# Sliding-window attention and a squared-ReLU FFN on one core: attention woven between the FFN's matmul groups, longer load runs for q and k, and the mask applied after the exponential

## Chip, cores, metric

The kernel runs on one core of a Trainium2 chip. The metric is the device time of one execution in microseconds (us). "Span" is the time from the first to the last instruction in one profiled execution; it is about 2 us shorter than the execution's time. PE is the tensor engine, DVE the vector engine, ACT the scalar engine, POOL the GpSimd engine, SP the engine that issues DMAs. The granted clock is the share of PE's full clock in the clock entries of a trace; where a trace has no entry, the views print 1.00.

## The reference

```python
# q, k, v: (8 batches, 8 heads, 576 tokens, 64), fp32, normal * 0.1
scores = q @ k.T / sqrt(64)
mask   = (0 <= i - j) & (i - j < 64)            # causal window of 64 keys
attn   = softmax(where(mask, scores, -1e9))
x      = (attn @ v) as (4608 tokens, 512)       # heads side by side
h      = maximum(x @ w_in, 0)                   # w_in  (512, 2048)
out    = (h * h) @ w_out                        # w_out (2048, 512), fp32 out
```

The inputs make the scores about 0.01 in size. So the softmax is nearly uniform, and the comparison with the reference hardly sees which query meets which key inside the window.

## The kernel before

A batch has four head pairs; two heads of 64 fill the 128 rows of the PE array. The FFN works on blocks of 512 tokens: "up" is 16 groups of four matmuls (hps), "down" is four groups of sixteen (ops). Each batch's attention is a stage of its own, followed by the FFN blocks whose tokens are then complete.

```python
# stageA(b, hp): load, cast, transpose, copy out of PSUM
for hh in range(2):
    nc.sync.dma_start(out=dst[:, 0:NC, hh, :],            # 64 floats = 256 B runs
        in_=src[b, h0 + hh, 0:NC * P, :].rearrange("(c p) d -> p c d", p=P))
    ...
nc.vector.tensor_copy(out=q16[:], in_=q_st[:])            # and k16: casts on DVE
... # 5 transposes each into qT_ps, kT_ps
nc.scalar.activation(out=qT[:], in_=qT_ps[:], func=AF.Copy, scale=1.0 / float(D) ** 0.5)
nc.scalar.activation(out=kT[:], in_=kT_ps[:], func=AF.Copy, scale=1.0)

# stageB: 18 score matmuls, then
nc.vector.tensor_tensor(out=pm[:, 0:512], in0=scA[hh][:], in1=mask_flat[:, 0:512], op=ALU.add)
nc.vector.tensor_tensor(out=pm[:, 512:S], in0=scB[hh][:], in1=mask_flat[:, 512:S], op=ALU.add)
nc.scalar.activation(out=pm[:], in_=pm[:], func=AF.Exp)
...
# main loop
for b in range(B):
    ctxs = [stageA(b, hp) for hp in range(HP)]
    if b == 0: load_w_in()                  # 16 x 256 KB through 3 staging buffers
    pms = [stageB(ctxs[hp]) for hp in range(HP)]
    for hp in range(HP): stageC(hp, ctxs[hp], pms[hp], x_sb)     # values, quotient
    if b == 0: load_w_out()
    ...                                     # transpose x into xT
    emit_ffn_blocks(ready)                  # the whole up stage, then the whole down stage
```

The softmax here doesn't subtract the row's maximum and nothing guards it: scores larger than these inputs give would overflow.

## Time and profile before

| | before |
|---|---|
| time, median of 3 runs | 444.27 us (444.19 to 444.62) |
| span of the profiled run | 443.0 us |
| attention of batch 2 complete | about 153.5 us |
| from there, one batch with one FFN block | 45.7 us |
| mean granted clock | 0.884 |

The 45.7 us come from the timeline: the first up matmul after batch 2's attention starts at 153.5 us and that after batch 7's at 382.0 us, five batches later. This start is what "attention complete" means for the kernel before. (The copy of the batch's last tokens into xT starts slightly later there, at 153.7 and 382.9 us, because the next block does not need them.)

From the page of the kernel before: busy time by engine; the granted clock in 40 slices of the span, in tenths; and the chain of waits by engine (the work that ended last, followed backwards).

```profile
PE 369.1 (83%) x2784; PEld 190.6 (43%) x2784; DVE 232.4 (52%) x648; ACT 217.3 (49%) x357; POOL 76.7 (17%) x241
...
PEclk9999999955999599967996799769975999599999
...
PE 61%; DVE 20%; DMA 7%; SPq 6%; issue 3%; ACT 1%; POOL 0%; DVEq 0%; POOLq 0%; ACTq 0%
```

PE looks 83% busy, but the clock row has a dip to 5 or 6 tenths once per batch. A "busy" PE at a low clock is not full speed. A batch cut into stages shows it. The next fence is the windows view: start and end of the stretch; its length; busy us of PE, PE weight load, DVE, ACT, POOL with the number of instructions; granted clock; share of the 16 DMA engines; GB/s.

```profile
core 0: us, PE busy (x) PEld busy (x) DVE busy (x) ACT busy (x) POOL busy (x), PEclk, DMA share, GB/s
138.00:153.50 15.50, 11.65 (x196) 8.52 (x196) 13.54 (x56) 10.55 (x19) 4.81 (x14) 0.67 0.56 132
153.50:169.00 15.50, 15.46 (x65) 6.67 (x65) 12.27 (x21) 9.76 (x16) 4.07 (x13) 0.89 0.54 123
169.00:184.00 15.00, 15.00 (x79) 7.07 (x78) 1.37 (x4) 4.67 (x8) 1.87 (x7) 1.00 0.56 145
```

The first stretch is attention: DVE is busy for 13.54 of 15.50 us, PE waits between small matmuls, and the clock is granted at 0.67. The second is the up stage, which starts at the low clock (0.89 on average); the third is mainly the down stage at full clock. The copies of the transposed q and k out of PSUM (busy us, mean ns of one, idle time before and its releaser):

```profile
L172 ACT ACTIVATE qT<-qT_ps 128x576 f16<-128x576 f16 x32 | 21.6, 675 | 19.3 <-PE qT_ps L164 19.3
L174 ACT ACTIVATE kT<-kT_ps 128x576 f16<-128x576 f16 x32 | 21.9, 685 | 8.1 <-PE kT_ps L164 8.1
```

### The profile page before, as it was taken

The page shows a single profiled execution, that of the slowest core. Times are in us where ns is not written, and L with a number is a line of the kernel's source. Part 1 is how long each engine was busy: PE and PEld are TensorE (multiplying, and loading weights), DVE is VectorE, ACT ScalarE, POOL GpSimd, SP SyncE. Part 2 cuts the span into 40 slices and gives each one's busy share as a digit, 9 for nine tenths or more (in the row PEclk, how much of TensorE's full clock was granted, in tenths as well). Part 3 has the DMA queues.
Part 4 walks back from the last instruction along what each step waited for, and adds up shares of the span by engine and source line. Part 5 has one row for each costly group of instructions (what it writes and reads, how often), then busy time and mean ns, then how long its engine had stood idle before and what let it go on. Part 6 is the DMA issues. An engine that isn't in the chain of part 4 may idle for free.

```text
span 443.0 us, 8064 instructions
## 1 busy us (share of the span) xinstructions
PE 369.1 (83%) x2784; PEld 190.6 (43%) x2784; DVE 232.4 (52%) x648; ACT 217.3 (49%) x357; POOL 76.7 (17%) x241
## 2 busy tenths in 40 slices
PE   1245698657999799969997999799988998899996
PEld 0133243343445444544455444534464445444442
DVE  0237780058823972396429751966088705788100
ACT  2233186652746465555537452826182717277311
POOL 5230201032312322232014200430011000000000
PEclk9999999955999599967996799769975999599999
DMA  4657888555556555645424532553130010000112
GB/s 112 138 131 203 228 217 232 165 133 115 122 133 164 122 122 132 170 108 117 117 83 111 121 82 83 122 117 70 71 80 0 2 68 28 1 1 1 47 72 73
DMA packets 126569, 46.68 MB, mean 105 GB/s; under 512 B 117824, under 2 KB 117824, under 8 KB 126528
## 3 DMA queue, kind: packets, MB, share of 16 engines
q1 hardware_dynamic: 126528, 46.17, 40.8%
q8 instruction: 22, 0.36, 0.3%
q14 instruction: 19, 0.16, 0.1%
HBM read 36.70 MB, written 9.44 MB: 104 GB/s over the span
## 4 chain that ended last, share of the span: by engine, by line
PE 61%; DVE 20%; DMA 7%; SPq 6%; issue 3%; ACT 1%; POOL 0%; DVEq 0%; POOLq 0%; ACTq 0%
PE hps L104 30%; PE ops L119 25%; DVE x_sb L251 4%; SPq L141 3%; SPq L146 3%; PE kT_ps L159 2%; DMA ws<-in_moe_w_in_dram 2%; DMA k_st<-in_k_dram 2%; PE qT_ps L159 2%; DVE x_sb L257 2%; DMA q_st<-in_q_dram 1%; DVE xT L284 1%; DVE rden L246 1%; ACT w_out_sb L94 1%; DMA ws_603<-in_moe_w_out_dram 1%
## 5 line engine op out<-in xcount | busy, mean ns | idle before, releaser
L104 PE MATMUL hps<-xT,w_in_sb 128*128 128x512 f16 x576 | 143.2, 416 | 5.2 <-DVE xT L284 5.1
L112 DVE TENSOR_SCALAR hrelu<-hps 128x512 f32<-128x512 f32 x144 | 99.1, 691 | 35.7 <-PE hps L104 33.1
L104 PEld LDWEIGHTS <-w_in_sb 128*128 128x128 f16 x576 | 60.6, 105 | 84.9 <-issue 27.9
L126 ACT ACTIVATE osb<-ops 128x512 f32<-128x512 f32 x36 | 21.3, 599 | 83.2 <-PE ops L119 83.2
L177 ACT ACTIVATE v_ev<-v_st 128x640 f16<-128x640 f32 x32 | 23.2, 730 | 27.8 <-DMA v_st<-in_v_dram 27.8
L182 POOL COPY v_od<-v_ev 64x512 f16<-64x512 f16 x32 | 19.5, 610 | 97.7 <-ACT v_ev L177 97.3
L278 PE MATMUL xt_ps<-ident,x_sb 128*128 128x128 f16 (+1 forms) x160 | 23.5, 293 | 11.0 <-DVE x_sb L251 6.0
L172 ACT ACTIVATE qT<-qT_ps 128x576 f16<-128x576 f16 x32 | 21.6, 675 | 19.3 <-PE qT_ps L164 19.3
L139 POOL MEMSET q_st<- 64x128 f32 x32 | 10.7, 334 | 98.2 <-DVE q_4818 L153 23.0
L174 ACT ACTIVATE kT<-kT_ps 128x576 f16<-128x576 f16 x32 | 21.9, 685 | 8.1 <-PE kT_ps L164 8.1
L202 PEld LDWEIGHTS <-kT 64*128 64x128 f16 x576 | 17.8, 104 | 12.0 <-issue 12.0
L278 PEld LDWEIGHTS <-x_sb 128*128 128x128 f16 (+1 forms) x160 | 14.0, 126 | 20.1 <-DVE x_sb L251 9.9
L184 POOL COPY v_od<-v_ev 64x512 f16<-64x512 f16 x32 | 19.7, 616 | 1.7
L119 PE MATMUL ops<-w_out_sb,h_654 128*128 128x512 f16 x64 | 15.0, 378 | 2.3 <-ACT w_out_sb L94 2.1
L114 ACT ACTIVATE h_3934<-hrelu 128x512 f16<-128x512 f32 x16 | 10.0, 630 | 11.1 <-DVE hrelu L112 10.9
L114 ACT ACTIVATE h_4590<-hrelu 128x512 f16<-128x512 f32 x16 | 10.1, 630 | 10.9 <-DVE hrelu L112 10.9
L114 ACT ACTIVATE h_5246<-hrelu 128x512 f16<-128x512 f32 x16 | 10.1, 630 | 10.6 <-DVE hrelu L112 10.6
L114 ACT ACTIVATE h_3278<-hrelu 128x512 f16<-128x512 f32 x16 | 10.0, 629 | 10.0 <-DVE hrelu L112 10.0
L119 PE MATMUL ops<-w_out_sb,h_5246 128*128 128x512 f16 x64 | 14.5, 379 | 0.0
L119 PE MATMUL ops<-w_out_sb,h_5247 128*128 128x512 f16 x64 | 14.5, 379 | 0.0
L139 POOL MEMSET k_st<- 64x128 f32 x32 | 9.4, 295 | 26.6 <-DMA v_st<-in_v_dram 3.3
L119 PE MATMUL ops<-w_out_sb,h_1310 128*128 128x512 f16 x64 | 14.0, 379 | 0.0
(1140 smaller groups left out, 615.1 us busy)
## 6 DMA issues: line engine op xcount, KB each, us to landing
out_dram<-osb SPq DMA_DIRECT2D x36, 256.0 KB, 2.0
q_st<-in_q_dram SPq DMA_DIRECT2D x64, 128.0 KB, 2.5
k_st<-in_k_dram SPq DMA_DIRECT2D x64, 128.0 KB, 2.4
v_st<-in_v_dram SPq DMA_DIRECT2D x64, 128.0 KB, 2.4
ws<-in_moe_w_in_dram SPq DMA_DIRECT2D x16, 256.0 KB, 4.1
q_st<-in_q_dram SPq DMA_DIRECT2D x64, 16.0 KB, 2.3
k_st<-in_k_dram SPq DMA_DIRECT2D x64, 16.0 KB, 2.2
v_st<-in_v_dram SPq DMA_DIRECT2D x64, 16.0 KB, 2.2
```

Of the source, the lines that this page charges most:

```text
L104: nc.tensor.matmul(hps[:], w_in_sb[:, c, f * P:(f + 1) * P], xT[:, c, g * 512:(g + 1) * 512], start=(c == 0), stop=(c == DMC - 1),)
L112: nc.vector.tensor_scalar(out=hrelu[:], in0=hps[:], scalar1=0.0, scalar2=None, op0=ALU.max)
L114: nc.scalar.activation(out=h2s[g][:, f, :], in_=hrelu[:], func=AF.Square)
L119: nc.tensor.matmul(ops_t[:], h2s[g][:, f, ts * P:(ts + 1) * P], w_out_sb[:, f, :], start=(f == 0), stop=(f == FFC - 1),)
L126: nc.scalar.activation(out=osb[:], in_=ops_t[:], func=AF.Copy, scale=OUT_SCALE)
L139: nc.gpsimd.memset(dst[TAIL:P, NC, :, :], 0.0)
L172: nc.scalar.activation(out=qT[:], in_=qT_ps[:], func=AF.Copy, scale=1.0 / float(D) ** 0.5)
L174: nc.scalar.activation(out=kT[:], in_=kT_ps[:], func=AF.Copy, scale=1.0)
L177: nc.scalar.activation(out=v_ev[:, :, :, 0:D], in_=v_st[:].rearrange("p c h d -> p h c d"), func=AF.Copy, scale=1.0,)
L182: nc.gpsimd.tensor_copy(out=v_od[0:64, :, :, 0:D], in_=v_ev[64:P, :, 0:NC, 0:D])
L184: nc.gpsimd.tensor_copy(out=v_od[64:P, :, :, 0:D], in_=v_ev[0:64, :, 1:NCH, 0:D])
L278: nc.tensor.transpose(out=xt_ps[:, c, 0:nrow], in_=x_sb[0:nrow, sc, c * P:(c + 1) * P], identity=ident[0:nrow, 0:nrow],)
```

## The change

The intent has three parts.

- **Weave.** The attention of batch g+1 is cut into steps, and they are emitted evenly between the up groups of block g and the down groups of block g-1. PE takes its matmuls in program order, so with this order it has FFN work between two dependent attention steps. PSUM is divided: three buffers for up, two for down, three for attention. The casts of q, k and v move to POOL, and q and k leave PSUM on ACT and DVE, one each.
- **Longer runs.** Partition p takes the six consecutive tokens 6p to 6p+5, so one run of q or k is 1.5 KB in place of 256 B. After the transposes the tokens stand as (r, p), and they must be (p, r). The copy out of PSUM does this: it reads contiguously and writes with a stride of six fp16 elements, 12 bytes.
- **Exponential first.** ACT takes exp straight from PSUM; then DVE takes the minimum with an fp16 mask (65504 to keep, 0 to drop), all in SBUF.

The rewrite changes more than the three parts named: the squared ReLU is now relu on ACT and a fused max and multiply on DVE (before: maximum on DVE, square on ACT), v is loaded for all eight heads at once, the last 64 queries of the four pairs are handled in one step, and the memsets of padding are gone.

The core of the diff; the old stages go, and the rest of the new code is left out ("..."):

```diff
+def weave(*streams):          # merge lists of steps evenly by relative position
+    keyed = []
+    for s, steps in enumerate(streams):
+        n = len(steps)
+        for i, step in enumerate(steps):
+            keyed.append(((i + 0.5) / n, s, i, step))
+    keyed.sort(key=lambda e: e[:3])
+    return [e[3] for e in keyed]
 ...
+    wst = ctx.enter_context(tc.tile_pool(name="wst", bufs=3))      # weight staging
+    ps_up  = ... bufs=3      ps_out = ... bufs=2      ps_att = ... bufs=3     (PSUM)
 ...
+                nc.sync.dma_start(                                 # 1.5 KB runs
+                    out=st[:].rearrange("p h r d -> p h (r d)"),
+                    in_=src[b, 2 * hp:2 * hp + 2].rearrange("h (p r) d -> p h (r d)", r=RT))
+                nc.gpsimd.tensor_copy(out=d16[:].rearrange("p r h d -> p h r d"), in_=st[:])
 ...
+                dT = attw.tile([P, PT, RT], FP16, name=f"{nm}T", tag=f"{nm}T", bufs=5)
+                if nm == "q":
+                    nc.scalar.activation(out=dT[:].rearrange("p t r -> p r t"), in_=ps[:],
+                                         func=AF.Copy, scale=1.0)
+                else:
+                    nc.vector.tensor_copy(out=dT[:].rearrange("p t r -> p r t"), in_=ps[:])
 ...
+                nc.scalar.activation(out=pm[:], in_=sc[hh][:], func=AF.Exp,
+                                     scale=1.0 / float(D) ** 0.5)
+                nc.vector.tensor_tensor(out=pm[:], in0=pm[:], in1=mask[:], op=ALU.min)
 ...
+        loads = [lambda hp=hp: load_qk(hp) for hp in range(HP)]
+        loads.insert(1, load_v)                                    # pair 0, all of v, pair 1 ...
+        for hp in range(HP):
+            steps.append(lambda hp=hp: transposes(hp))
+            steps.append(lambda hp=hp: scores(hp, pms[hp]))
+            if hp > 0:
+                steps.append(lambda hp=hp - 1: values(hp, pms[hp], holds[hp]))
+                steps.append(lambda hp=hp - 1: to_xT(hp, holds[hp]))
 ...
+    for g in range(NTB + 1):
+        streams = []
+        if g < NTB:    streams.append(ffn_up(g))
+        if g > 0:      streams.append(ffn_out(g - 1))
+        if g + 1 < B:  streams.append(nxt[1])                      # attention steps of g+1
+        if g == 0:     streams.append(w_out_steps)
+        if g + 2 < B:  nxt = attention(g + 2); streams.append(nxt[0])   # its loads
+        for s in weave(*streams):
+            s()
```

## The prediction

> **What bounds the kernel now.** The chain of waits is PE 61%, DVE 20%, DMA 7%. By stage windows, a steady batch takes about 46 us and alternates two stages. (a) Attention, 138.0 to 153.5 us: PE waits on DVE's mask adds (0.68 us each), quotients and copies; granted clock 0.67. (b) FFN, 153.5 to 184 us: PE-bound, 64 up matmuls in 15.5 us and 64 down matmuls in 13.8 us (216 ns each). The down stage runs at clock 1.00, the up stage at 0.84 to 0.89 because it starts cold. The Trainium skill ("TensorE: Matmul & The Clock Gate", Part 1) says that the array drops to half clock after an idle window and recovers after sustained work[...]. Around this: the first FFN matmul at 50 us, w_out waits to 82 us, and batch 1's attention only ending at 107 us (its chain waits for loads and POOL copies). SP issues 420 DMAs at 0.51 to 0.59 us each.
>
> **What the change does.**
> - Moves batch g+1's attention between the FFN matmul groups of blocks g and g-1. PE, in order, always has FFN work between dependent attention steps (about 1.7 us of it), so the 15.5 us stage shrinks to its pure PE time at full clock. From warm pieces of the trace: 18 score matmuls 0.29 us, 5 transposes 0.45 us, 16 value matmuls about 0.5 us (cold). That is 48 + 20 transposes about 6, 72 scores 1.3, 72 values 2.2: about 9.5 us per batch (estimate).
> - FFN at 216 ns throughout: 27.6 us per block, no cold up stage.
> - Exp straight from PSUM removes the serial DVE add before ACT; the fp16 min in SBUF should cost about 0.4 us against 0.68 (estimate, with the ratio of 16-bit SBUF tensor_tensor in "VectorE: DVE Perf Modes", perf-mode tier table; no trace yet shows it).
> - DVE per block about 24 us (now 27), ACT 20 to 21 (now 24.5), POOL up to about 18 (casts of q, k, v added, memsets gone): all well under PE.
> - DMA issues fall from about 420 to 124, most q/k packets from 256 B to 1.5 KB. The same bytes.
>
> **Sum.** Start: batch 0's loads (3.5 MB at 200 to 230 GB/s) and POOL casts give attention 0 done near 29 us; w_in, in rounds of three buffers, near 35. Block 0 and block 1 are still held by loads (18.9 MB, about 82 us at 230 GB/s) and w_out casts: block 1 ends near 100 us. Then five full blocks at 27.6 + 9.5 + about 5 for PE switches and in-order stalls = 42 (210), two FFN-only blocks at 28.2 (56), last down stage 14.7, last eviction and store 3: 384 us. The steady blocks give about 4 us each; the larger part comes from the first two batches (now attention 2 would end at 154 us, then near 100).
>
> **Prediction: 384 us, 8 in 10 between 368 and 404.** Faster by over 2%: 0.97; within 2%: 0.02; slower: 0.01.
>
> **What would show it.** Granted clock 0.95 or more from about 60 us on; PE idle under 10% in blocks 2 to 8; block period 40 to 44 us; the DVE share of the chain of waits below 8%; mean of both FFN matmul groups' spacing near 216 ns; exp near 0.6 us, min near 0.4 us; first FFN matmul near 25 to 30 us.
>
> **What would make it wrong.** Higher: stride-6 fp16 writes of qT/kT slow on ACT/DVE; POOL casts of 96x768 over 1.5 us, so that attention waits for POOL; three PSUM buffers for attention too few, so that every step stalls PE; batch 0's serial casts of v before q1/k1 delaying the start; weights' three staging buffers. Lower: attention's matmuls hidden better than estimated, loads faster than 230 GB/s.

## The result and the profile after

| | before | after |
|---|---|---|
| median of 4 runs | 444.23 us (444.00 to 444.62) | 382.96 us (382.22 to 383.91) |
| ratio, 95% interval | | 0.8628 (0.8609 to 0.8647): faster |
| span of the profiled run | 443.0 us | 380.5 us |
| mean granted clock | 0.884 | 0.994 |
| attention of batch 2 complete | 153.5 us | 120.7 us |
| one batch with one FFN block, later | 45.7 us | 37.4 us |

A ratio is the mean time of one kernel's fast runs over that of the other kernel's in the same rounds; it is not quite the ratio of the medians quoted beside it.

The same three lines of the page after, with the next line of the page, the chain by line of the program:

```profile
PE 327.2 (86%) x2848; PEld 160.5 (42%) x2848; DVE 255.4 (67%) x468; ACT 215.0 (56%) x309; POOL 118.6 (31%) x178
...
PEclk9999998999999999999999999999999999999999
...
PE 60%; DVE 23%; ACT 6%; DMA 4%; issue 3%; POOL 2%; SPq 0%; ACTq 0%; POOLq 0%
PE ops L307 25%; PE hps L288 23%; DVE kT L171 15%; DMA ws<-in_moe_w_in_dram 3%; PE av L204 2%; ACT hrelu L293 2%; DVE x_sb L209 2%; PE xt_ps L216 2%; PE qT_ps L164 2%; PE kT_ps L164 2%; DMA v_st<-in_v_dram 1%; ACT w_out_sb L123 1%; ACT qT L168 1%; DVE h_601 L294 1%; DVE w_in_sb L110 1%
```

The dips of the clock row are gone. PE's busy time fell from 369.1 to 327.2 us for practically the same matrix work. But one line is new in the chain: the DVE copy of kT, L171, with 15% of the span. The two copies, by group:

```profile
L168 ACT ACTIVATE qT<-qT_ps 128x576 f16<-128x576 f16 x32 | 67.4, 2105 | 29.3 <-PE qT_ps L164 29.2
L171 DVE COPY kT<-kT_ps 128x576 f16<-128x576 f16 x32 | 66.7, 2086 | 14.4 <-PE kT_ps L164 13.7
```

The same 128x576 elements that took 675 and 685 ns now take 2105 and 2086 ns. By stage (columns as above; batch 0's attention, batch 1's, batch 2's, then one later block, then the last two blocks, which have no attention):

```profile
0.00:46.70 46.70, 19.15 (x228) 11.87 (x229) 26.09 (x58) 16.21 (x18) 22.38 (x39) 1.00 0.80 198
46.70:83.80 37.10, 29.73 (x294) 14.48 (x292) 29.60 (x56) 25.11 (x37) 21.04 (x31) 0.95 0.79 192
83.80:120.70 36.90, 31.55 (x321) 15.45 (x318) 29.71 (x55) 26.45 (x41) 16.47 (x23) 1.00 0.84 209
158.10:195.50 37.40, 35.55 (x345) 17.57 (x343) 29.35 (x55) 24.15 (x35) 14.13 (x22) 1.00 0.56 141
308.20:362.50 54.30, 54.30 (x254) 24.61 (x252) 21.45 (x31) 23.19 (x39) 0.00 (x0) 1.00 0.10 39
```

In a later block PE is busy for 35.55 of 37.40 us at clock 1.00. Before, a batch needed 45.7 us with 0.67 in its attention stage. The Trainium skill ("TensorE: Matmul & The Clock Gate", Part 1) says that the array drops to half clock after an idle window. The trace of the kernel before agrees only in part. In windows of 2 us the clock is at 0.50 from 144 to 156 us and back at 1.00 from 158, after some 3 us of up matmuls; but PE was never idle for more than 0.92 us in that stage, so no long idle stretch came before the dip. What the trace shows is that the dips lie in the stage of small matmuls with waits between them (PE busy for 11.65 of 15.50 us), and that the woven later blocks have none.

A caution about the 1.00 of the first stretch: the trace has no clock entry before 51.8 us (kernel before: 54.4), and the means 0.994 and 0.884 count that time as 1.00. The six transposes of one q tile, in batch 0's attention and in a later block (timeline: start us, us, engine, line, operation):

```profile
24.18 0.69 PE L164 MATMUL qT_ps<-ident,q_156 96*128 96x96 f16 x6
...
195.27 0.43 PE L164 MATMUL qT_ps<-ident,q_2415 96*128 96x96 f16 x6
```

They start every 80 ns in batch 0's attention and every 42 ns in the later block, so PE was at about half speed in the former.

**Where the time came from.** At the end of batch 2's attention the kernel before has also done the down stage of block 1 (13.8 us), which the changed kernel still has to do. So the start gave 153.5 - 13.8 - 120.7 = 19.0 us. The five batches that follow gave 228.5 - 187.0 = 41.5 us, 8.3 each. The end gave the remaining 2.0 of 62.5 us of span. (With the copy of the last tokens as the mark in both kernels the split is 19.2, 42.2 and 1.1.)

What the long copy does in a later block, from the timeline (start us, duration, engine, line, operation; in brackets the idle time before and what ended it):

```profile
195.53 0.42 PE L164 MATMUL kT_ps<-ident,k_2419 96*128 96x96 f16 x6
195.79 1.03 PE L288 MATMUL hps<-xT,w_in_sb 128*128 128x512 f16 x4
195.99 2.09 DVE L171 COPY kT<-kT_ps 128x576 f16<-128x576 f16 x1 [0.18 <-PE kT_ps L164]
196.65 1.03 PE L307 MATMUL ops<-w_out_sb,h_2345 128*128 128x512 f16 x4
198.14 0.20 PE L181 MATMUL sc_2969<-qT,kT 64*128 64x64 f16 x1 [0.46 <-DVE kT L171]
```

Between the transposes and the scores, PE has one up group and one quarter of a down group to do. The copy takes 2.09 us and is ready a little too late: PE idles 0.46 us. That is 1.85 us for the four pairs of a block, the whole idle time of PE there (37.40 - 35.55).

And at the start there is no FFN work to hide it. Pieces of the chain of waits, in order of time (start us, us, what):

```profile
2.22 5.19 DMA v_st<-in_v_dram
...
10.12 1.37 POOL v_ev_107 L152 x2
...
14.85 0.77 POOL q_148 L143
...
17.93 2.08 DVE kT L171
...
24.09 6.48 DMA ws<-in_moe_w_in_dram
...
```

Three suspects show here: the casts of v come before those of head pair 1 on POOL; the copies of kT; and loads of w_in that wait for one of three staging buffers.

### The profile page after: what moved, and what is told of

Its sections match the earlier page's. It is cut to its first block, busy times and chain, and to the rows that moved or that the text cites. A ratio compares the mean times of both kernels' runs of the same rounds, so it can differ in the third digit from the quotient of the medians.

```text
span 380.5 us, 7267 instructions
## 1 busy us (share of the span) xinstructions
PE 327.2 (86%) x2848; PEld 160.5 (42%) x2848; DVE 255.4 (67%) x468; ACT 215.0 (56%) x309; POOL 118.6 (31%) x178
## 4 chain that ended last, share of the span: by engine, by line
PE 60%; DVE 23%; ACT 6%; DMA 4%; issue 3%; POOL 2%; SPq 0%; ACTq 0%; POOLq 0%
PE ops L307 25%; PE hps L288 23%; DVE kT L171 15%; DMA ws<-in_moe_w_in_dram 3%; PE av L204 2%; ACT hrelu L293 2%; DVE x_sb L209 2%; PE xt_ps L216 2%; PE qT_ps L164 2%; PE kT_ps L164 2%; DMA v_st<-in_v_dram 1%; ACT w_out_sb L123 1%; ACT qT L168 1%; DVE h_601 L294 1%; DVE w_in_sb L110 1%
## 5 line engine op out<-in xcount | busy, mean ns | idle before, releaser
L288 PE MATMUL hps<-xT,w_in_sb 128*128 128x512 f16 x576 | 155.6, 392 | 1.4 <-DVE h_601 L294 1.3
L293 ACT ACTIVATE hrelu<-hps 128x512 f32<-128x512 f32 x144 | 91.0, 637 | 88.8 <-PE hps L288 59.8
L168 ACT ACTIVATE qT<-qT_ps 128x576 f16<-128x576 f16 x32 | 67.4, 2105 | 29.3 <-PE qT_ps L164 29.2
L171 DVE COPY kT<-kT_ps 128x576 f16<-128x576 f16 x32 | 66.7, 2086 | 14.4 <-PE kT_ps L164 13.7
L288 PEld LDWEIGHTS <-w_in_sb 128*128 128x128 f16 x576 | 50.1, 100 | 49.2 <-issue 5.7
L181 PEld LDWEIGHTS <-kT 64*128 64x128 f16 x512 | 10.1, 99 | 41.2 <-DVE kT L171 40.1
L209 DVE TENSOR_TENSOR x_sb<-av,rden 128x256 f16<-128x256 f32 x64 | 25.0, 419 | 0.3
L294 DVE SCALAR_TENSOR_TENSOR h_4658<-hps,hrelu 128x512 f16<-128x512 f32 x16 | 11.1, 692 | 16.7 <-ACT hrelu L293 16.7
L294 DVE SCALAR_TENSOR_TENSOR h_4867<-hps,hrelu 128x512 f16<-128x512 f32 x16 | 11.1, 692 | 16.6 <-ACT hrelu L293 16.6
L152 POOL CAST v_ev_108<-v_st 128x512 f16<-128x512 f32 (+1 forms) x20 | 12.4, 631 | 30.6 <-DMA v_st<-in_v_dram 20.8
L216 PE MATMUL xt_ps<-ident,x_sb 128*128 128x128 f16 x128 | 13.3, 230 | 9.9 <-DVE x_sb L209 9.9
L152 POOL CAST v_ev_107<-v_st 128x512 f16<-128x512 f32 (+1 forms) x20 | 12.3, 622 | 22.7 <-DMA v_st<-in_v_dram 14.1
L307 PE MATMUL ops<-w_out_sb,h_601 128*128 128x512 f16 x64 | 18.5, 379 | 0.1
L307 PE MATMUL ops<-w_out_sb,h_2345 128*128 128x512 f16 x64 | 16.6, 379 | 0.0
L307 PE MATMUL ops<-w_out_sb,h_3529 128*128 128x512 f16 x64 | 16.6, 379 | 0.0
L307 PE MATMUL ops<-w_out_sb,h_1753 128*128 128x512 f16 x64 | 16.6, 379 | 0.0
L307 PE MATMUL ops<-w_out_sb,h_1161 128*128 128x512 f16 x64 | 16.6, 379 | 0.0
L307 PE MATMUL ops<-w_out_sb,h_2937 128*128 128x512 f16 x64 | 16.6, 379 | 0.0
L307 PE MATMUL ops<-w_out_sb,h_4121 128*128 128x512 f16 x64 | 16.4, 379 | 0.0
L307 PE MATMUL ops<-w_out_sb,h_4658 128*128 128x512 f16 x64 | 16.4, 379 | 0.0
```

The source lines that it names most:

```text
L152: nc.gpsimd.tensor_copy(out=v_ev[0:n, c, :, 0:D], in_=st[0:n])
L168: nc.scalar.activation(out=dT[:].rearrange("p t r -> p r t"), in_=ps[:], func=AF.Copy, scale=1.0)
L171: nc.vector.tensor_copy(out=dT[:].rearrange("p t r -> p r t"), in_=ps[:])
L181: nc.tensor.matmul(sc[hh][:, j, :], kTs[hp][r0:r0 + 64, ks:ks + P], qTs[hp][r0:r0 + 64, j * 64:(j + 1) * 64], start=True, stop=True)
L209: nc.vector.tensor_tensor(out=x_sb[:, :, hh, :], in0=av[:, :, 0:D], in1=rden[:].to_broadcast([P, NC, D]), op=ALU.mult)
L216: nc.tensor.transpose(out=xt[:, c, :], in_=hold["x"][:, c, :, :], identity=ident[:])
```

## The experiments

All edits are against the changed kernel unless said otherwise. "Attention 0 / 1 / 2 done" is the start, in the timeline, of the copy of the batch's last tokens into xT. "Later block" is the period of one woven block. The runs were made in three sets, each on another chip; the medians of the kernel before were 443.95, 444.13 and 443.89 us in them, so ratios and medians can be compared across sets. The moments in the last two columns come from one profiled execution each.

| run | us | ratio to before | attention 0 / 1 / 2 done | later block |
|---|---|---|---|---|
| changed kernel | 382.96 | 0.8628 | 46.7 / 83.8 / 120.7 | 37.4 |
| e1_flat | 358.27 | 0.8063 | 43.4 / 73.8 / 107.8 | 35.3 |
| e3_runs256 | 371.56 | 0.8363 | 40.4 / 83.5 / 121.5 | 35.3 |
| e4_noweave | 486.69 | 1.0958 | 46.6 / 99.9 / 154.5 | 54.7 |
| e6_wst7 | 378.28 | 0.8502 | 44.7 / 80.6 / 116.0 | 37.4 |
| e2_readstride | 359.03 | 0.8093 | 44.8 / 76.1 / 107.6 | 35.3 |
| e5_addmask | 379.69 | 0.8570 | 47.7 / 80.5 / 115.3 | 38.0 |
| e7_order | 372.47 to 374.53 | 0.8410 | no fast profile | |
| e10_comb | 373.2 | 0.8411 | 41.4 / 76.9 / 116.7 | 36.3 |
| e11_weaveonly | 368.99 | 0.8305 | 41.4 / 82.8 / 120.3 | 35.3 |
| e12_read_wst7 | 355.46 | 0.8000 | 41.2 / 73.7 / 105.9 | 35.3 |
| e13_read_vlate | 350.42 | 0.7886 | 38.2 / 67.6 / 99.1 | 35.3 |
| e14_read_addmask | 358.06 | 0.8070 | 47.0 / 75.9 / 106.9 | 35.3 |

### Copies out of PSUM without the stride (e1_flat), token order wrong on purpose

```diff
-                dT = attw.tile([P, PT, RT], FP16, ...)
+                dT = attw.tile([P, RT, PT], FP16, ...)
-   ... out=dT[:].rearrange("p t r -> p r t"), in_=ps[:]
+   ... out=dT[:], in_=ps[:]
```

> The changed kernel, but the copies of qT and kT out of PSUM write contiguously (token order is then wrong, so the result is wrong on purpose; same shapes and counts). Theory A: the stride-6 writes, 2.1 us per copy, cause the one regular PE wait of the woven blocks (0.46 us, four times per block) and a part of the long start. Then a copy costs about 0.7 us, a block falls from 37.4 to about 35.5 us, the start by 5 to 10 us, total 360 to 368 us. Rival B: the copies are hidden and another wait (the three PSUM buffers, the in-order ACT and DVE queues) takes their place: blocks stay above 37 us, total above 376 us.

Measured: 358.27 us, ratio 0.8063 (0.8025 to 0.8101), a little below the range of theory A. The two groups:

```profile
L168 ACT ACTIVATE qT<-qT_ps 128x576 f16<-128x576 f16 x32 | 20.8, 651 | 29.8 <-PE qT_ps L164 29.8
...
L171 DVE COPY kT<-kT_ps 128x576 f16<-128x576 f16 x32 | 14.6, 457 | 18.7 <-PE kT_ps L164 18.2
```

Same shapes, same types, same engines; only the write pattern differs. The stride costs a factor of 3.2 on ACT (2105 over 651) and 4.6 on DVE (2086 over 457), and the two copies together 24.7 us of the kernel's time. The scores of this kernel meet the wrong keys, yet the check against the reference passed: as said above, it does not see the order of tokens inside q and k. So a pass proves nothing about the order here, and the index mapping of every later kernel was followed by hand.

### The stride on the reading side (e2_readstride), result right

```diff
-   ... out=dT[:].rearrange("p t r -> p r t"), in_=ps[:]
+   ... out=dT[:], in_=ps[:].rearrange("p r t -> p t r")
```

This is the same permutation of the same elements: SBUF is written contiguously, and PSUM is read with the stride.

> Same load runs and right token order as the changed kernel, but the reordering moved from the write side of the qT and kT copies to the read side: stride-96 reads from PSUM, contiguous 2-byte writes to SBUF. If the 2.1 us come from the strided SBUF writes, a copy costs 0.7 to 1.0 us and the total is 358 to 364 us, like the contiguous-copy run. If any stride on either side costs the same (per-element access), a copy stays near 2.1 us and the total near 383.

Measured: 359.03 us, ratio 0.8093 (0.8066 to 0.8120). The two groups, and one later block in the windows view:

```profile
L171 DVE COPY kT<-kT_ps 128x576 f16<-128x576 f16 x32 | 24.2, 757 | 15.5 <-PE kT_ps L164 14.9
...
L168 ACT ACTIVATE qT<-qT_ps 128x576 f16<-128x576 f16 x32 | 20.8, 651 | 31.3 <-PE qT_ps L164 31.3
```

```profile
142.80:178.10 35.30, 35.30 (x346) 17.59 (x343) 24.00 (x55) 19.01 (x35) 14.15 (x22) 1.00 0.58 146
```

The strided read costs ACT nothing (651 ns, as without any stride) and DVE 300 ns (757 against 457). In the block PE is now busy for 35.30 of 35.30 us: the only bound left there is PE's own work, and e1 with its still faster copies has the same 35.3. Of the 23.7 us of span saved, 5 x 2.1 = 10.5 lie in the five blocks and 13.1 in the start (120.7 to 107.6).

Note how this compares with the chain of waits, which had the kT copy at 15% of 380.5 us, 57 us. Cutting this copy by two thirds, and that of qT with it, gave 23.7. So a line's share of the chain is no forecast of what shortening it gives back: behind it stand other waits that end almost as late, here PE's own work.

### 256 B runs with the weave (e3_runs256)

```diff
-    in_=src[b, 2*hp:2*hp+2].rearrange("h (p r) d -> p h (r d)", r=RT)       # one DMA
+    for h in range(2):  ... in_=src[b, 2*hp+h].rearrange("(r p) d -> p r d", r=RT)
     # token = r*96 + p, so the copies out of PSUM are contiguous and the order is right
```

> Undoes the 1.5 KB runs alone: q and k are loaded with 256 B runs (token = r*96+p), so that the copies of qT and kT are contiguous and the result right. Theory A: the long runs bought nothing on this path, the bytes and staging are the same; time equals that of the contiguous-copy run within 3 us, about 362 to 370. Rival B: 256 B packets slow the first 80 us, where loads limit: 5 us or more over the contiguous-copy run, DMA share higher in the start.

Measured: 371.56 us, ratio 0.8363 (0.8335 to 0.8390). It has e1's copies and later block (35.3 us), so against e1 it shows what the runs do (with twice as many DMA issues for q and k): 371.6 - 358.3 = 13.3 us, all in the start. Batch 1's attention, first in this kernel, then in e1 (windows view):

```profile
40.40:83.50 43.10, 31.39 (x289) 16.26 (x287) 27.33 (x63) 18.55 (x34) 19.98 (x30) 0.77 0.94 188
```

```profile
43.40:73.80 30.40, 26.47 (x288) 13.08 (x286) 23.51 (x56) 18.55 (x35) 19.94 (x30) 0.95 1.04 224
```

The DMA engines are busy in both (0.94 and 1.04 of their time), but they move 188 GB/s with 256 B runs and 224 with 1.5 KB. The Trainium skill ("DMA: Bandwidth & Descriptors", "Why small descriptors are slow (HBM only)") puts this down to a fixed overhead per packet; the two rates agree in direction. So the long runs, with the halved number of issues, are worth 13 us where loads bind, and nothing later. As the change implements them they also bring the strided writes, which cost 24.7. The part as a whole lost 11.4 us: the changed kernel has 382.96, this one 371.56.

### The weave undone (e4_noweave)

```diff
-    for g in range(NTB + 1):  for s in weave(ffn_up(g), ffn_out(g-1), nxt[1], ...): s()
+    for g in range(NTB):      up(g); then out(g) with the loads; then all attention steps of g+1
```

> Undoes the weaving alone: emission order attention, up, down of each batch as in the kernel before; loads, copies, exp and min as in the changed kernel. Theory A: weaving is what pays; without it attention is a serial stage of 18 to 24 us per batch (2.1 us copies in a chain, half clock), a block takes 46 to 52 us and the total is 450 to 500 us, slower than the kernel before. Rival B: the cheaper operations (exp from PSUM, fewer DMA issues, no memsets) carry the gain: total below 430 us.

Measured: 486.69 us, ratio 1.0958 (1.0921 to 1.0994), slower than the kernel before by 42 us and than the changed one by 103.7. The clock row of its page, one later block in the windows view, and a wait from its timeline:

```profile
PEclk9999989999856996599856996599856996589999
```

```profile
154.50:209.20 54.70, 42.41 (x344) 22.27 (x341) 29.71 (x56) 24.55 (x35) 14.59 (x22) 0.78 0.30 85
```

```profile
186.91 0.61 PE L181 MATMUL sc<-qT,kT 64*128 64x64 f16 x16 [2.42 <-DVE kT L171]
```

The dips are back. The block is 54.7 us, 27.2 of FFN and some 27.5 of attention alone: PE now waits out the whole copy of kT (2.42 us here; 47.0 us over the run in the waits view). That it is slower than the kernel before is probably because these attention steps, with 2.1 us copies and only three PSUM buffers, were made to be hidden; the old stage was better suited to run by itself. How much of the 42 us is owed to which of the two was not tried.

### The weave with the other two parts undone (e11_weaveonly)

The edits of e3_runs256 and of e5_addmask (below) together.

> Both other named parts undone together: 256 B runs (contiguous copies) and the float32 mask added on DVE before exp; the weaving and the rest of the rewrite stay. Theory A: weaving carries the gain; near 368 to 374 us, no slower than the changed kernel at 383. Rival B: the parts only pay together: 385 us or more.

Measured: 368.99 us, ratio 0.8305 (0.8265 to 0.8345). The weave without the other two parts, with contiguous copies, beats the changed kernel by 14 us and the kernel before by 75. So the weave, with all else of the rewrite that this run keeps (the division of PSUM, the casts on POOL, the other form of the squared ReLU, the loads of v), carries more than the whole gain, and the other two parts together took something back. What the weave alone is worth with short copies was not measured: e4 takes it out of the kernel with the long ones.

### The additive mask before the exponential (e5_addmask, e14_read_addmask)

```diff
-                nc.scalar.activation(out=pm[:], in_=sc[hh][:], func=AF.Exp, scale=...)
-                nc.vector.tensor_tensor(out=pm[:], in0=pm[:], in1=mask[:], op=ALU.min)
+                nc.vector.tensor_tensor(out=pm[:], in0=sc[hh][:], in1=mask32[:], op=ALU.add)
+                nc.scalar.activation(out=pm[:], in_=pm[:], func=AF.Exp, scale=...)
```

> Undoes exp-then-min alone: DVE adds a float32 mask from PSUM, ACT takes exp in SBUF, all else as in the changed kernel. Theory A: PE bounds the woven block and the masking has three steps of slack, so the block stays at 37.4 us and only the start moves; total 383 to 388 us. Rival B: DVE (29.3 us busy of 37.4) is near its limit in order, +2 us of adds per block delays the kT copies that PE waits for: block 38.5 us or more, total above 390 us.

> Strided reads with contiguous writes, and the float32 mask add from PSUM in place of the fp16 min in SBUF. With strided writes the add was 3 us faster in all: block +0.6, start -5.4. Theory A: the min is slow only while POOL works (0.71 against 0.43 us), that is in the start; here DVE has more slack, so start about -2 to -4 us, blocks +0 to 0.3: 355 to 359 us. Rival B: the start's gain was a matter of instruction order: 358 to 364 us.

Measured: 379.69 us, ratio 0.857 (0.8523 to 0.8617), against 0.8628 (0.8609 to 0.8647) of the changed kernel: the intervals just overlap, so a gain from the undoing is unclear. In the kernel with the strided read: 358.06 against 359.03 us, ratio 0.807 (0.8043 to 0.8097) against 0.8093: the same within the intervals. So this part is worth about nothing. In e5 that is a trade, which neither theory foresaw: attention 2 is done 5.4 us earlier (115.3 against 120.7), and each later block is 0.6 us longer (38.0 against 37.4). The minimum was cheaper than the add, but not always. In e5 the add takes:

```profile
L194 DVE TENSOR_TENSOR pm<-sc,mask 128x512 f16<-128x512 f32 x64 | 41.0, 682 | 1.8 <-PE sc L189 1.8
```

The minimum in the changed kernel, once with POOL idle and once with POOL at work (two places of the timeline):

```profile
37.59 0.41 DVE L188 TENSOR_TENSOR pm_424<-pm_424,mask 128x512 f16<-128x512 f16 x1
...
101.14 0.82 POOL L143 CAST k_1235<-k_st 96x768 f16<-96x768 f32 x1 [0.46 <-DMA k_st<-in_k_dram]
101.30 1.50 DVE L188 TENSOR_TENSOR pm_1424<-pm_1424,mask 128x512 f16<-128x512 f16 x1
101.91 0.61 POOL L152 CAST v_ev_108<-v_st 128x512 f16<-128x512 f32 x1
```

Of the 64 minimums of this shape, the 45 that overlap no POOL instruction take 0.43 us on average, and the 19 that do take 0.71, up to 1.50. The add from PSUM in e5 takes 0.68 either way. The Trainium skill says both things. "VectorE: DVE Perf Modes" (the perf-mode tier table) gives a two-tensor operation twice the rate when all its tensors are 16-bit in SBUF, and none of that from PSUM; 0.43 against 0.68 agrees in direction. "GPSIMD Engine Reference" (section 1, Specifications) has POOL's SBUF interface shared with the vector engine, with "contention with DVE instructions in a 2-port perf mode or with two SBUF inputs"; the minimum has two SBUF inputs, the add has one, and only the minimum is slower beside POOL. This is read from what overlaps in time; no run changed POOL's work to test it.

### More weight staging buffers (e6_wst7, e12_read_wst7)

Weight tiles go round 7 buffers (4 of wst, and the 3 output buffers that are unused at that time) in place of 3.

```diff
-            ws = wst.tile([P, FQ], FP32, name="ws", tag="ws")          # bufs=3
+            ws = wtile([P, FQ], "ws")      # i % 7 < 4: wst (bufs=4), else the 3 of opool
```

> The changed kernel with seven staging buffers for the weights in place of three (four own, three of the output's). Theory A: the start (block 2 begins at 122 us, where I estimated 100) is held by rounds of three weight loads that wait for casts queued behind attention on DVE and ACT; with seven, block 2 begins at 108 to 115 us and the total is 368 to 376 us. Rival B: the start is held by attention 0's own chain (POOL casts of v before q1, 2.1 us copies) and by DMA bandwidth: total within 3 us of 383.

> Strided reads with contiguous writes, and seven staging buffers for the weights. The buffers gave about 4.7 us in the changed kernel. Theory A: the start is still held by rounds of weight loads: 352 to 356 us. Rival B: with faster copies the start is bound by DMA bandwidth (share 0.96 to 0.98 from 45 to 108 us at 228 to 244 GB/s): within 2 us of 359.

Measured: alone, 378.28 us (375.32 to 379.30), ratio 0.8502 (0.8457 to 0.8547), 4.7 us less than the changed kernel, all in the start, and between what the two theories said. On top of the strided read, 355.46 us against 359.03, 3.6 less; in the profiled execution, the slowest of its six (356.85), attention 2 is done 1.7 us earlier. So three buffers did hold up the weights, as the prediction feared, but for less than the copies did.

### Another order of the steps (e7_order), and a combination (e10_comb)

In e7_order the value step of the pair before stands between the transposes and the scores of a pair, which leaves more PE time for the long copies. e10_comb adds the seven buffers and loads head pair 1 before v.

```diff
             steps.append(lambda hp=hp: transposes(hp))
-            steps.append(lambda hp=hp: scores(hp, pms[hp]))
             if hp > 0:
                 steps.append(lambda hp=hp - 1: values(hp, pms[hp], holds[hp]))
+            steps.append(lambda hp=hp: scores(hp, pms[hp]))
+            if hp > 0:
                 steps.append(lambda hp=hp - 1: to_xT(hp, holds[hp]))
```

> The changed kernel with one swap in the weave: values of the head pair before come between transposes and scores, so that the 2.1 us copies have two FFN rounds (3.5 us) instead of one. Theory A: the regular wait of PE for the kT copy goes in three of the four head pairs, a block falls from 37.4 to 35.7 to 36.2 us, total 372 to 378 us. Rival B: the three PSUM buffers then stall PE elsewhere (scores wait for the value tiles to be read): block 37 us or more, total above 380.

> Seven weight buffers, the swap in the weave, and batch loads in the order pair 0, pair 1, v, pair 2, pair 3, so that POOL casts pair 1 before v. Gains expected to add: 4.7 us from the buffers, about 8 from the swap, 3 to 5 from the start: total 366 to 372 us. If the start is bound by DMA bandwidth, the last two overlap and the total is 370 to 376.

Measured, e7: three runs of 372.47, 372.66 and 374.53 us, ratio 0.841 (0.8374 to 0.8446). A fourth run, the one that was profiled, took 659.32 us and counts as slow. Its profile shows where that time went: FFN matmuls start 443 ns apart (median, all through the run) where the changed kernel has 216, while the copies of qT and kT take 2093 and 2077 ns as ever. So PE alone was slow, though the clock reads 1.00: this trace has no clock entry at all. What held PE back is not known. About 10 us come back by order alone (382.96 against the fast median of 372.66), which agrees with the waits on the kT copy being a matter of where the scores stand. e10: 373.2 us, ratio 0.8411 (0.8383 to 0.8439), not faster than e7, although it has two more edits of which each helps elsewhere. Its later block is 36.3 us and its attention 2 is done at 116.7 us. Gains in the start do not add up while the long copies are there. From 41.4 to 116.7 us the waits view names first the value matmuls that wait for ACT's copy of qT (4.8 us in five waits); no run tested it.

### Pair 1 before v, with the strided read and seven buffers (e13_read_vlate)

```diff
-        loads.insert(1, load_v)
+        loads.insert(2, load_v)
```

> The kernel before this one, with the loads of head pair 1 ahead of v, so that POOL's casts of v no longer hold PE (waits for POOL 13 us in all in the start). Theory A: attention 0 ends 3 to 5 us earlier and so does everything: 348 to 353 us. Rival B: bandwidth: no change beyond 1.5 us.

Measured: 350.42 us (349.59 to 350.99, 4 runs), ratio 0.7886 (0.7861 to 0.7910), the best of all: 32.5 us under the changed kernel. Against e12 it is 5.0 us, and attention 2 is done 6.8 us earlier. Its stages (windows view: attention 0, 1, 2, and a later block):

```profile
0.00:38.20 38.20, 18.44 (x224) 11.27 (x224) 19.22 (x59) 10.17 (x18) 18.19 (x32) 0.96 0.90 230
38.20:67.60 29.40, 27.56 (x298) 13.66 (x299) 23.81 (x56) 20.35 (x39) 19.78 (x29) 1.00 1.08 238
67.60:99.10 31.50, 30.73 (x315) 14.91 (x313) 23.34 (x54) 20.87 (x40) 18.35 (x27) 1.00 0.96 230
134.60:169.90 35.30, 35.30 (x346) 17.58 (x343) 24.18 (x56) 19.03 (x35) 17.07 (x26) 1.00 0.69 170
```

The DMA engines are now nearly always busy in the start (0.90 to 1.08 of their time, at 230 to 238 GB/s), and PE is fully busy later. In the stretches of batches 1 and 2 PE is nearly always busy as well (27.56 of 29.40 and 30.73 of 31.50 us), so little is left there. In the first 38.2 us PE works for 18.44; fewer bytes, or weights that arrive later, would be the next thing to try there, and neither was.

## Why the prediction was right or wrong

The total was right: 384 us predicted, 382.96 measured. Its split was not. The prediction's sum against the profiled span:

| term of the sum | predicted | changed kernel | e13_read_vlate |
|---|---|---|---|
| until the five woven blocks begin (attention 2 done) | 100 | 120.7 | 99.1 |
| five woven blocks | 5 x 42 = 210 | 5 x 37.4 = 187.0 | 5 x 35.3 = 176.5 |
| two FFN-only blocks, last down stage, last store | 74 | 72.8 | 72.9 |
| sum | 384 | 380.5 | 348.5 |

Two errors of about 20 us, of opposite sign, cancelled: that the total was hit within about 1 us is luck.

**The start: "block 1 ends near 100 us", measured 120.7.** The terms that failed are the copies of qT and kT, the weights' buffers and the order of the casts. The prediction named all three under "What would make it wrong". Its sum had POOL's casts ("attention 0 done near 29 us") and the rounds of three buffers (w_in "near 35"), both too short: attention 0 is done at 46.7 us and the last cast of w_in ends at 49.3. It had nothing for the long copies. The runs give them sizes: going from one kernel to the next, attention 2 is done 13.1 us earlier with the copies' stride moved to the reading side (e2), 1.7 with seven staging buffers (e12), and 6.8 with pair 1 ahead of v on POOL (e13). Together that is 21.6 us, and it brings the start to 99.1. This is the predicted 100, but not by the predicted path, as attention 0 is done at 38.2 us in e13 and not at 29. The sizes are rough: by the medians the last two steps are 3.6 and 5.0 us, seven buffers alone gave 4.7 us in e6, and e13 moves the loads of pair 1 as well as their casts.

**The blocks: "27.6 + 9.5 + about 5", measured 37.4.** The mechanism was right: PE-bound at full clock. The FFN alone takes 54.3 / 2 = 27.2. In e2, where PE has no gaps, the block is 35.3, so attention's share of PE is about 8.2, not 9.5; that estimate came partly from cold matmuls. The term "about 5 for PE switches and in-order stalls" was mis-sized: it is 2.1 in the changed kernel, of which 1.85 are the waits for the kT copy, and none in e2.

**"The steady blocks give about 4 us each; the larger part comes from the first two batches": wrong, and the other way round.** The blocks gave 8.3 each, 41.5 of 62.5 us; the start gave 19.0.

**"Exp straight from PSUM removes the serial DVE add before ACT; the fp16 min ... about 0.4 us": size right, effect wrong.** 0.43 us without POOL. But a serial DVE operation is still there, behind the exponential in place of ahead of it, and undoing this part cost nothing (e5, e14). With the short copies neither sets the length of a later block (35.3 in e2 and in e14); with the long ones the add made it 0.6 us longer (e5).

**"DMA issues fall from about 420 to 124, most q/k packets from 256 B to 1.5 KB": right but for the count.** The pages list 416 issues of loads before and 136 after, with 36 stores in each. Packets fell from 126,569 to 60,642. The gain was not costed in the sum; it is 13 us, in the start, and only if the copies do not pay for it (e3 against e1).

**The views named in advance.** Right: clock of 0.95 or more from 60 us on (1.00 but for 3.4 us at 62.0); PE idle under 10% (35.55 of 37.40 busy in a later block); FFN matmuls near 216 ns; exp near 0.6 us (0.60); first FFN matmul near 25 us (25.15). Wrong: block period of 40 to 44 us (37.4); DVE under 8% of the chain (23%, of which 15 are the kT copy). DVE per block was to be 24 us and was 29.4; with the strided read it is 24.0, so the whole excess was the copy. ACT was to be 20 to 21 and was 24.2, for the same reason (19.0 in e2).

## What to carry to other kernels

Give an in-order PE other work between dependent small steps: here that took an attention stage of 15.5 us at clock 0.67 down to about 8 us of PE time at full clock (in e2). When fp16 data have to be permuted on their way out of PSUM, try the stride on the reading side and write SBUF contiguously, as e2 did here, and look at the time of every copy whose access pattern a change of load layout has altered. A forecast that hits the total should be checked term by term, because here two errors of 20 us hid three small edits that were worth 32 us together.

## What the Trainium skill lacked or had wrong

- "SBUF — State Buffer" (Door 1: The DMA port swizzle) says that SBUF has 16-byte cachelines, that at least two hits on a line are needed, and that how far one can stride for free depends on the type: 8 for bf16. Read as a stride of up to 8 elements, this did not hold here. Writes of fp16 with a stride of 6 elements (12 bytes, inside that limit if fp16 counts as bf16, though two neighbours do not always share a line) were not free: 2105 against 651 ns on ACT and 2086 against 457 ns on DVE for 128x576. "Advanced Engine Details and Errata" (SBUF Cachelines) is nearer with its "performance penalty" for a different cacheline per access, but gives no size. That cachelines are the cause was not tested; the runs show only the stride's cost.
- No page says that the reading side of such a copy is the cheap one. A strided PSUM read (192 bytes from element to element) cost ACT nothing (651 against 651 ns) and DVE 300 ns (757 against 457). What "Advanced Engine Details and Errata" says of slow non-contiguous PSUM patterns concerns matmuls.
- "GPSIMD Engine Reference" (section 1) names the contention with DVE but gives no size for a pair like this one: a 128x512 fp16 minimum took 0.43 us without POOL, 0.71 on average with it, and up to 1.50.
